# A streamed decode-attention kernel: one A head's V per set moves from TensorE to GpSimd and VectorE, the softmax minimum reaches all rows by one product, and the stream is walked in another order

## The chip, the cores and the metric

The kernel runs on one core of a Trainium2 chip. The metric is the device time of one execution in microseconds (us). Engines: PE is TensorE, DVE is VectorE, ACT is ScalarE, POOL is GpSimd, SP is SyncE, whose queue issues the transfers. All data are fp32.

## What is computed

One query row `x` (448 wide) goes through two attention blocks with cached keys and values, and a sigmoid gate mixes the two outputs:

```
A: 16 heads, each with its own K and V (8192 rows x 256)
B: 16 query heads on 8 K/V heads (two query heads share one K/V)
per block:  q = x @ wq;  p = softmax(q . K * 256**-0.5);  o = p @ V;  y = concat(o) @ wo
g = sigmoid(sum(x * gate_w));   out = g * yA + (1 - g) * yB
```

K and V are 24 + 24 arrays of 8 MB, about 403 MB of the 432 MB that are read; the rest are `wq` and `wo`. Each element is used for one or two products, so the work is a stream.

## The kernel before

The work is cut into 8 sets (`s`). A set has two A heads (`r` = 0 and 1) and one B head (`r` = 2, with two query rows). Each K and each V is cut into 4 tiles (`t`) of 128 partitions x 4096 elements (16 cache rows of 256 in each partition). A set also has one `wq` item (its columns of both query weights) and one `wo` item (its rows of both output weights). The last set's `wo` is cut into `first` and `rest`. The names below are like v7.0.3: V, set 7, head 0, tile 3; k6.1.3 is the last key tile of head 1 of set 6.

The list `order()` writes the items one after another, and this is the order in which the host has laid them in DRAM, in which they are loaded, and in which the instructions of every engine stand. The stream is loaded without regard to item borders, in *fills* of 16384 elements a partition (8.39 MB, four tiles), into a ring of three slots (`load`, L112 to L119; SP's queue). There are 53 fills, numbered 0 to 52: 50 full ones (0 to 49), one of 6144 elements (fill 50, 3072 KB), and two cut into five parts each (fill 51: the last V tiles and `first`; fill 52: `rest`). Fill n+3 goes into the slot of fill n, and its load waits until everything that reads or writes fill n there is done. The first three loads are issued at once.

What each item costs on the engines:

- A keys (`scores_a`, L232): DVE multiplies the tile by q in place (L239; q lies in PSUM) and sums each row of 256 (L240). After the last tile the smallest of the 64 scores of each partition (`low`, L243).
- B keys (`scores_b`): the tile lies transposed, and PE multiplies it by q (8 products of 512 columns a tile, each two instructions in the trace); after the last tile DVE takes `low` from PSUM (L258).
- `softmax` (L261), after the last key tile of a head: PE turns `low` into one row (`ident`), DVE takes its minimum (L269), PE spreads that to all rows (`ones`, or `alt` for B's two query rows), ACT copies it (L277) and takes the exponential (L281, L288). For B, DVE then transposes the weights (L283).
- V (`attend`): PE, 8 products a tile (`o<-slot,p` or `o<-slot,pr`), summed in PSUM. After the last tile come `sums` (sum of the weights over all partitions by PE, its reciprocal on DVE, L300), `take` (ACT copies the PSUM, L333) and one item later `narrow` (PE adds up the four row groups, `sm<-pick_a,ob`, and DVE scales, L349).
- `wo`: `emit` adds the set's eight 448-wide products to `Y` in PSUM. After that of set 6, `quarters` copies `Y` (DVE, L367) and folds it to four rows.

PE and DVE are in order: an instruction that waits holds everything behind it on its engine.

Of the kernel before, what the change touches and what calls it, by code (L numbers as in the profile page):

```python
# [36 lines left out]
TAIL = [[11 * UNIT, 10 * UNIT, EARLY * D + 2 * UNIT, 4 * UNIT, 2 * UNIT], [2 * D, D, D, 336, 112]]  # L37


def order():  # L40

    out = [("wq", 0, 0, 0)]
    for s in range(NS):
        def k(r, *ts):
            return [("k", s, r, t) for t in ts]

        def v(r, *ts, of=s):
            return [("v", of, r, t) for t in ts]

        if s == 0:  # L50
            out += k(0, 0) + k(2, 0, 1) + k(0, 1) + k(2, 2) + k(0, 2) + k(2, 3) + k(0, 3)
            out += v(2, 0, 1) + k(1, 0) + v(2, 2, 3) + k(1, 1) + v(0, 0, 1) + k(1, 2) + v(0, 2)
            out += k(1, 3) + v(0, 3) + [("wq", 1, 0, 0)]
            continue
        out += k(0, 0) + v(1, 0, 1, of=s - 1) + k(0, 1) + v(1, 2, 3, of=s - 1)
        out += k(0, 2) + k(2, 0, 1) + k(0, 3) + k(2, 2, 3) + [("wo", s - 1, 0, 0)]
        out += k(1, 0) + v(0, 0, 1) + k(1, 1) + v(0, 2, 3)
        if s < NS - 1:
            out += [("wq", s + 1, 0, 0)] + k(1, 2) + v(2, 0, 1) + k(1, 3) + v(2, 2, 3)
        else:  # L60
            out += k(1, 2) + v(2, 0) + k(1, 3) + v(2, 1, 2, 3) + v(1, 0, 1, 2)
            out += [("first", s, 0, 0)] + v(1, 3) + [("rest", s, 0, 0)]
    return out
# [14 lines left out]
def kernel(  # L78
# [21 lines left out]
    def mm(o, l, r, start=False, stop=False):  # L100
        nc.tensor.matmul(o, l, r, start=start, stop=stop, skip_group_check=True)  # L101
# [130 lines left out]
    def scores_a(s, r, t, a):  # L232
        if t == 0:
            S[s, r] = small.tile([P, NT * ROWS], F32, name="s", bufs=3)
        q = QA[s][:, r * DH:(r + 1) * DH]
        for d, n, v in pieces(a, TILE):
            j, n = d // DH, n // DH
            v = v.rearrange("p (j d) -> p j d", d=DH)
            nc.vector.tensor_tensor(v, v, q[:, None, :].to_broadcast([P, n, DH]), op=OP.mult)  # L239
            nc.vector.tensor_reduce(S[s, r][:, t * ROWS + j:t * ROWS + j + n], v, axis=AX.X, op=OP.add)  # L240
        if t == NT - 1:
            low = small.tile([P, 1], F32, name="low")
            nc.vector.tensor_reduce(low, S[s, r], axis=AX.X, op=OP.min)  # L243
            OF[s, r] = low

    def scores_b(s, t, a):
        if t == 0:
            SC[s] = ps_sc.tile([P, UNIT], F32, name="sc")
        sc = SC[s]
        for d, n, v in pieces(a, TILE):  # L250
# [5 lines left out]
        if t == NT - 1:  # L256
            low = small.tile([P, 1], F32, name="low")
            nc.vector.tensor_reduce(low, sc, axis=AX.X, op=OP.min)  # L258
            OF[s, 2] = low

    def softmax(s, r):  # L261
        turned = ps_s.tile([1, P], F32, name="sm")
        mm(turned, OF.pop((s, r)), ident, start=True, stop=True)
        m = 2 if r == 2 else 1
        least = small.tile([1, 2], F32, name="least")
        view = turned
        if r == 2:
            view = turned.rearrange("p (g r) -> p g r", g=NG)[:, :, :R].rearrange("p g (t m) -> p m g t", m=2)
        nc.vector.tensor_reduce(least[:, :m], view, axis=AX.XY if r == 2 else AX.X, op=OP.min)  # L269
        all_rows = ps_s.tile([P, 1], F32, name="sm")  # L270
        if r == 2:
            for k in range(2):
                mm(all_rows, alt[:, k], least[:, k:k + 1], start=(k == 0), stop=(k == 1))
        else:
            mm(all_rows, ones[:1, :], least[:, :1], start=True, stop=True)
        bias = small.tile([P, 1], F32, name="bias")
        nc.scalar.activation(bias, all_rows, AF.Copy)  # L277
        rs = small.tile([P, 1], F32, name="rs", bufs=4)
        if r == 2:
            px = small.tile([P, UNIT], F32, name="px")  # L280
            nc.scalar.activation(px, SC.pop(s), AF.Exp, bias=bias, scale=-1.0, accum_out=rs)  # L281
            pr = small.tile([P, UNIT], F32, name="pr", bufs=1)
            nc.vector.transpose(pr.rearrange("p (q r k) -> p q k r", r=BLK, k=2),  # L283
                                px.rearrange("p (q k c) -> p q k c", c=BLK, k=2))
            PR[s, r] = pr
        else:
            p = small.tile([P, NT * ROWS], F32, name="p")
            nc.scalar.activation(p, S.pop((s, r)), AF.Exp, bias=bias, scale=-1.0, accum_out=rs)  # L288
            PR[s, r] = p
        RS[s, r] = rs  # L290

    def sums(s, r):
# [4 lines left out]
        for k in range(m):
            mm(z[:, k:k + 1], par[:, k] if r == 2 else ones, rs, start=True, stop=True)
# [6 lines left out]
    def attend(s, r, t, a):  # L305
        if t == 0:
# [4 lines left out]
        for d, n, v in pieces(a, TILE):  # L311
            for b in range(d // UNIT, (d + n) // UNIT):
                g = b % NG
                c = b * UNIT - d
# [75 lines left out]
    nxt = SLOTS  # L390
    gone = 0
    last = len(items) - 1
    for i, ((kind, s, r, t), a) in enumerate(items):
        if kind == "wq":
            qrow = queries(s, a)
            after(i, turn, s, qrow)
        elif kind == "k":
            if r == 2:
                scores_b(s, t, a)
            else:  # L400
                scores_a(s, r, t, a)
            if t == NT - 1:
                softmax(s, r)
        elif kind == "v":
            attend(s, r, t, a)
            if t == NT - 1:
                end = i == last - 1
                if not end:
# [1 line left out]
                take(s, r, 2 if end else 1)  # L410
                if not end:
                    after(i + 1, narrow, s, r)
        elif kind == "wo":
# [102 lines left out]
```

## Time and profile before

| | |
|---|---|
| three runs | 1010.61 us median (1009.96 to 1010.9) |
| the profiled execution | 1009.79 us, span 1007.7 us |
| read from DRAM | 432.02 MB, 429 GB/s over the span |
| PE busy / mean granted clock | 492.8 us (49%) / 0.725 |
| DVE busy | 596.9 us (59%) |
| ACT, POOL busy | 37.9 us, 0.7 us |
| chain that ended last | DMA 61%, DVE 22%, PE 16% of the span |

The profile is of one execution, whose span is 2.1 us shorter than its time and whose time is 0.8 us under the median of the three runs. The numbers of the groups in it (lines of the kernel, engine, output and inputs, partitions x elements) have a mean duration in ns. In a timeline row the first number is the start, the second the time from there to the end of the row's last instruction; in square brackets is how long the engine had been idle and what ended that. A stage row has, after the length, busy time and number of instructions on PE, PEld (its weight loads), DVE, ACT and POOL, then the granted PE clock, the DMA share and GB/s.

### The profile page before, as it was taken

The numbers are of one execution on the slowest core, as the hardware profiler recorded it, in microseconds if no ns is written. First come the engines' busy times: TensorE is split into PE (matmuls) and PEld (weight loads), VectorE is DVE, ScalarE is ACT, GpSimd is POOL, SyncE is SP. The second block draws the span as 40 slices with busy tenths as digits, with TensorE's granted clock in tenths as the row PEclk, the third lists the DMA queues.
The fourth block names the chain that finished last, engine by engine and source line by source line (L and its number), as shares of the span: only waits on it lengthen the run. The fifth ranks groups of instructions, "written<-read, shape, count | busy, mean of one in ns | idle before, by whom it ended". The sixth has DMA issues, their size and how long they took to land.

```text
span 1007.7 us, 6321 instructions
## 1 busy us (share of the span) xinstructions
PE 492.8 (49%) x2843; PEld 148.1 (15%) x2843; DVE 596.9 (59%) x294; ACT 37.9 (4%) x107; POOL 0.7 (0%) x6
## 2 busy tenths in 40 slices
PE   1615482554435563445442566345634366544628
PEld 0201120111111211011110121111211112111102
DVE  1686767527766467652776646755277762675581
ACT  0000000000000000000000000000000000000000
POOL 0000000000000000000000000000000000000000
PEclk9857686777777777577777776766767677776658
DMA  9999999999999999999999999999999999999997
GB/s 416 416 455 419 443 425 424 447 427 442 425 425 442 432 435 440 432 430 427 440 430 445 427 440 425 430 442 422 453 420 440 430 432 440 424 448 427 432 418 296
DMA packets 8962, 432.42 MB, mean 429 GB/s; under 512 B 1256, under 2 KB 1640, under 8 KB 1896
## 3 DMA queue, kind: packets, MB, share of 16 engines
q1 hardware_dynamic: 8792, 432.02, 99.1%
q8 instruction: 22, 0.36, 0.1%
q14 instruction: 4, 0.03, 0.0%
q10 hardware_dynamic: 144, 0.00, 0.0%
HBM read 432.02 MB, written 0.00 MB: 429 GB/s over the span
## 4 chain that ended last, share of the span: by engine, by line
DMA 61%; DVE 22%; PE 16%; issue 0%; ACT 0%; SPq 0%
DMA slot<-in_stream_dram 61%; DVE s L240 11%; DVE slot L239 11%; PE o L101 6%; PE sc L101 4%; PE sm L101 3%; PE q L101 3%; DVE least L269 0%; DVE low L243 0%; PE Y L101 0%; DVE qb L230 0%; ACT px L281 0%; DVE pr L283 0%; DVE low L258 0%; ACT qrow L222 0%
## 5 line engine op out<-in xcount | busy, mean ns | idle before, releaser
L239 DVE TENSOR_TENSOR slot<-slot,q 128x4096 f32<-128x4096 f32 (+6 forms) x78 | 284.1, 3642 | 70.2 <-DMA slot<-in_stream_dram 70.2
L240 DVE TENSOR_REDUCE s<-slot 128x16 f32<-128x4096 f32 (+6 forms) x78 | 285.0, 3654 | 2.7
L101 PE MATMUL o<-slot,p 128*2 128x512 f32 (+1 forms) x1028 | 162.2, 743 | 185.5 <-DMA slot<-in_stream_dram 185.5
L101 PE MATMUL sc<-slot,qb 128*32 128x512 f32 x512 | 98.0, 857 | 68.1 <-DMA slot<-in_stream_dram 67.8
L101 PE MATMUL sm<-ident,low 128*1 128x128 f32 x48 | 13.0, 369 | 180.5 <-DVE low L243 162.0
L101 PE MATMUL o<-slot,pr 128*4 128x512 f32 x512 | 84.0, 773 | 29.1 <-DMA slot<-in_stream_dram 28.9
L300 DVE RECIPROCAL rz<-sm 128x1 f32<-128x1 f32 (+1 forms) x24 | 4.0, 167 | 130.4 <-PE sm L101 130.4
L101 PEld LDWEIGHTS o<-slot,p 128*2 128x2 f32 x1028 | 29.5, 97 | 301.6 <-DMA slot<-in_stream_dram 199.8
L349 DVE TENSOR_TENSOR ocs<-sm,rz 128x2 f32<-128x2 f32 (+2 forms) x25 | 3.9, 154 | 73.5 <-PE sm L101 73.4
L258 DVE TENSOR_REDUCE low<-sc 128x1 f32<-128x512 f32 x8 | 5.5, 690 | 63.8 <-PE sc L101 63.8
L101 PE MATMUL q<-slot,xr 128*128 128x512 f32 (+1 forms) x80 | 33.5, 567 | 11.7 <-DMA slot<-in_stream_dram 11.7
L101 PEld LDWEIGHTS sc<-slot,qb 128*32 128x32 f32 x512 | 20.2, 146 | 128.7 <-DMA slot<-in_stream_dram 77.3
L101 PEld LDWEIGHTS sm<-ident,low 128*1 128x1 f32 x48 | 2.3, 80 | 206.2 <-issue 96.0
L101 PE MATMUL sc<-slot,xr 128*1 128x512 f32 (+1 forms) x80 | 30.2, 525 | 0.0
L333 ACT ACTIVATE ob<-o 128x512 f32<-128x512 f32 (+1 forms) x24 | 14.1, 588 | 396.4 <-PE o L101 396.4
L101 PEld LDWEIGHTS o<-slot,pr 128*4 128x4 f32 x512 | 14.7, 100 | 84.0 <-issue 48.7
L277 ACT ACTIVATE bias<-sm 128x1 f32<-128x1 f32 x24 | 4.1, 171 | 477.0 <-PE sm L101 477.0
L101 PEld LDWEIGHTS q<-slot,xr 128*128 128x128 f32 x80 | 16.3, 214 | 25.7 <-DMA slot<-in_stream_dram 12.6
L101 PE MATMUL sm<-pick_a,ob 128*128 128x1 f32 x124 | 17.2, 259 | 3.1 <-ACT ob L333 2.9
L101 PE MATMUL Y<-slot,ocs 128*1 128x448 f32 (+3 forms) x178 | 17.3, 505 | 0.0
L101 PEld LDWEIGHTS sm<-pick_a,ob 128*128 128x128 f32 x124 | 15.9, 200 | 7.1 <-ACT ob L333 4.0
L269 DVE TENSOR_REDUCE least<-sm 1x1 f32<-1x128 f32 (+1 forms) x24 | 5.9, 245 | 16.0 <-PE sm L101 16.0
(64 smaller groups left out, 136.3 us busy)
## 6 DMA issues: line engine op xcount, KB each, us to landing
slot<-in_stream_dram SPq DMA_DIRECT2D x1, 3072.0 KB, 26.4
slot<-in_stream_dram SPq DMA_DIRECT2D x1, 2816.0 KB, 16.7
slot<-in_stream_dram SPq DMA_DIRECT2D x1, 2560.0 KB, 22.4
slot<-in_stream_dram SPq DMA_DIRECT2D x1, 1184.0 KB
slot<-in_stream_dram SPq DMA_DIRECT2D x1, 1024.0 KB, 26.7
slot<-in_stream_dram SPq DMA_DIRECT2D x50, 40.4
slot<-in_stream_dram SPq DMA_DIRECT2D x1, 512.0 KB, 27.5
slot<-in_stream_dram SPq DMA_DIRECT2D x1, 448.0 KB, 10.5
```

The lines of the kernel that those rows point to most:

```text
L101: nc.tensor.matmul(o, l, r, start=start, stop=stop, skip_group_check=True)
L239: nc.vector.tensor_tensor(v, v, q[:, None, :].to_broadcast([P, n, DH]), op=OP.mult)
L240: nc.vector.tensor_reduce(S[s, r][:, t * ROWS + j:t * ROWS + j + n], v, axis=AX.X, op=OP.add)
L258: nc.vector.tensor_reduce(low, sc, axis=AX.X, op=OP.min)
L269: nc.vector.tensor_reduce(least[:, :m], view, axis=AX.XY if r == 2 else AX.X, op=OP.min)
L277: nc.scalar.activation(bias, all_rows, AF.Copy)
L300: nc.vector.reciprocal(rz[:, :m], z[:, :m])
L333: nc.scalar.activation(ob[k][:, :n], o[:, k * n:(k + 1) * n], AF.Copy)
L349: nc.vector.tensor_tensor(ocs[:, e, :m], oc[e.start][:, e, :m], z.to_broadcast([P, e.stop - e.start, m]), op=OP.mult)
```

## The change

It has four parts.

1. V of one A head a set is no longer multiplied on PE. For the heads in `SPREAD` (head 0 of set 0, head 1 of sets 0 to 6: 8 heads, 32 tiles) POOL multiplies the tile in place by the weights (`spread`), and DVE later sums the 16 rows of each partition to 256 numbers (`settle`, reading with a step of 256 elements) and adds them to the head's `acc`. `settle` runs where a fill ends in the program, and ahead of each `wo`. `gather` then lets PE add up the partitions of `acc` in two products. The other 8 A heads and B stay with `attend`.
2. In `softmax` one product, whose stationary side is `low` repeated to 128 columns, puts all 128 values into every row; DVE takes each row's minimum straight from PSUM as the bias. For B it takes two minima a row and picks one by a mask (`half`). The second product and ACT's copy are gone. In `sums`, B takes one product of two columns in place of two.
3. `order()` deals the tiles of a set from three lists (A keys, PE's tiles, and V of the `SPREAD` head) by a string, so that they alternate. `wo` and `wq` of a set move near its end. The last six items (the four V tiles of head 1 of set 7, with `first` ahead of the fourth and `rest` behind it) keep their places, and so do the borders of the fills.
4. The loop walks an item that crosses from one fill into the next as two items, so that the load into the old slot and the `settle` of that fill stand between the two.

```diff
+SPREAD = {(0, 0)} | {(s, 1) for s in range(NS - 1)}
 def order():
...
-        out += k(0, 0) + v(1, 0, 1, of=s - 1) + k(0, 1) + v(1, 2, 3, of=s - 1)
...
+        walk = "kfkfkfkfkfvkfvkfvqkfv" if s == 0 else "kfkfvfkfkvfkfkvfkvfkfffof" if last else "kfkfvfkfvfkfvfkfvfkfkfoqkf"
+        for c in walk:
+            if c in "oq":
+                out.append(("wo", s - 1, 0, 0) if c == "o" else ("wq", s + 1, 0, 0))
+            else:
+                out.append({"k": keys, "f": fill, "v": mine}[c].pop(0))
...
     def softmax(s, r):
-        turned = ps_s.tile([1, P], F32, name="sm")
-        mm(turned, OF.pop((s, r)), ident, start=True, stop=True)
...
-            mm(all_rows, ones[:1, :], least[:, :1], start=True, stop=True)
-        bias = small.tile([P, 1], F32, name="bias")
-        nc.scalar.activation(bias, all_rows, AF.Copy)
+        every = ps_s.tile([P, P], F32, name="sm")
+        mm(every, OF.pop((s, r)).to_broadcast([P, P]), ident, start=True, stop=True)
+        bias = small.tile([P, 1], F32, name="bias")
         if r == 2:
...
+            nc.vector.tensor_reduce(least, view, axis=AX.XY, op=OP.min)
+            nc.vector.tensor_tensor(least, least, half, op=OP.mult)
+            nc.vector.tensor_reduce(bias, least, axis=AX.X, op=OP.add)
         else:
+            nc.vector.tensor_reduce(bias, every, axis=AX.X, op=OP.min)
...
+    def spread(s, r, t, a, lo, size):
...
+        for d, n, v in pieces(a + lo, size):
+            j, n = (lo + d) // DH, n // DH
+            w = PR[s, r][:, t * ROWS + j:t * ROWS + j + n]
+            v = v.rearrange("p (j d) -> p j d", d=DH)
+            nc.gpsimd.tensor_tensor(v, v, w[:, :, None].to_broadcast([P, n, DH]), op=OP.mult)
+            todo.append((s, r, v))
+    def settle():
+        for s, r, v in todo:
+            first = not ACC[s, r]
+            acc = small.tile([P, DH], F32, name="acc" if first else "more")
+            nc.vector.tensor_reduce(acc, v.rearrange("p j d -> p d j"), axis=AX.X, op=OP.add)
+            if first:
+                ACC[s, r].append(acc)
+            else:
+                nc.vector.tensor_tensor(ACC[s, r][0], ACC[s, r][0], acc, op=OP.add)
+        todo.clear()
+    def gather(s, r):
...
+        for e in range(2):
+            mm(oc[:, e, :1], acc[:, e * P:(e + 1) * P], gs[:, 0:1], start=True, stop=True)
...
         elif kind == "wo":
+            settle()
+            for r in range(2):
+                if (s, r) in SPREAD:
+                    sums(s, r)
+                    gather(s, r)
             emit(s, a)
...
-        while gone < len(ends) and a + SIZE[kind] >= ends[gone]:
+        while gone < len(ends) and a + lo + n >= ends[gone]:
             gone += 1
+            settle()
             if nxt < len(FILLS):
                 load(nxt)
```

What the fills hold near the end shows the new order best. Before, fills 46 to 49 hold: k7.2.0 (end), k7.2.1, k7.0.3, k7.2.2, k7.2.3 (start) | k7.2.3, wo6, k7.1.0, v7.0.0, v7.0.1 | v7.0.1 (end), k7.1.1, v7.0.2, v7.0.3, k7.1.2 (7/8) | k7.1.2 (end), v7.2.0, k7.1.3, v7.2.1, v7.2.2. Now fills 43 to 49 hold: v6.0.2, wo5, wq7, k6.1.3, v6.0.3 (3/4) | v6.0.3 (end), k7.0.0, k7.2.0, k7.0.1, k7.2.1 | k7.2.1 (end), v6.1.0, k7.2.2, k7.0.2, k7.2.3 | k7.2.3 (end), k7.0.3, v6.1.1, v7.2.0, k7.1.0 (3/4) | k7.1.0 (end), v7.2.1, k7.1.1, v6.1.2, v7.2.2 | v7.2.2 (end), k7.1.2, v7.2.3, v6.1.3, k7.1.3 (3/4) | k7.1.3 (end), v7.0.0, v7.0.1, v7.0.2, wo6. Fill 50 holds v7.2.2 (end), v7.2.3, v7.1.0 (3/8) before and wo6 (end), v7.0.3, v7.1.0 (3/8) now; fills 51 and 52 are the same.

DVE before, from the key tiles in fill 48 to the last softmax's minimum (`slot` is a tile in the ring, `s` the scores, `ocs` a head's finished output):

```order
L239 TENSOR_TENSOR slot<-slot,q 128x3584
L240 TENSOR_REDUCE s<-slot 128x14
L239 TENSOR_TENSOR slot<-slot,q 128x512
L240 TENSOR_REDUCE s<-slot 128x2
L349 TENSOR_TENSOR ocs<-sm,rz 128x2
L239 TENSOR_TENSOR slot<-slot,q 128x4096
L240 TENSOR_REDUCE s<-slot 128x16
L243 TENSOR_REDUCE low<-s 128x1
L269 TENSOR_REDUCE least<-sm 1x1
```

DVE now, fill 48 (k7.1.2, B's `sums` and output, three quarters of k7.1.3, the sum of v6.1.3) and what follows to the last softmax's minimum:

```order
L232 TENSOR_TENSOR slot<-slot,q 128x4096
L233 TENSOR_REDUCE s<-slot 128x16
L288 TENSOR_SCALAR both<-half,rs 128x2
L292 RECIPROCAL rz<-sm 128x2
L375 TENSOR_TENSOR ocs<-sm,rz 128x4
L232 TENSOR_TENSOR slot<-slot,q 128x3072
L233 TENSOR_REDUCE s<-slot 128x12
L338 TENSOR_REDUCE more<-slot 128x256
L342 TENSOR_TENSOR acc<-acc,more 128x256
L232 TENSOR_TENSOR slot<-slot,q 128x1024
L233 TENSOR_REDUCE s<-slot 128x4
L236 TENSOR_REDUCE low<-s 128x1
```

The last key tile's first three quarters have moved from fill 49 into fill 48, and ahead of its last quarter stand the sum over a tile that POOL has weighed and an addition. The same sum and addition stand at the end of fills 46 and 47, and the sum at that of fill 45.

PE before, from the last softmax (`sm<-ident,low`, `sm<-least,ones`) on:

```order
L101 MATMUL sm<-ident,low 1x128
L101 MATMUL sm<-least,ones 128x1
L101 MATMUL o_125<-slot,pr 4x512 x24
L101 MATMUL sm<-rs,par 128x1 x2
L101 MATMUL o_126<-slot,p 2x512 x8
L101 MATMUL sm<-pick_b,ob 128x2 x4
L101 MATMUL o_126<-slot,p 2x512 x16
L101 MATMUL sm<-rs,ones 128x1
L101 MATMUL Y<-slot,ocs 1x112 x12
L101 MATMUL o_126<-slot,p 2x512 x6
L101 MATMUL o_126<-slot,p 2x256 x4
```

PE now, from the same softmax (`sm<-ident,low`) to `quarters` (`Y<-ysum`) and the narrowing of head 0; behind it come `o_120<-slot,p` x21 and then the same rows as before from `sm<-rs,ones` on:

```order
L100 MATMUL sm<-ident,low 128x128
L100 MATMUL o_119<-slot,p 2x512 x24
L100 MATMUL sm<-rs,ones 128x1
L100 MATMUL sm<-gs,acc 128x1 x2
L100 MATMUL Y<-slot,ocs 1x448 x6
L100 MATMUL Y<-slot,ocs 1x384
L100 MATMUL Y<-slot,ocs 1x64
L100 MATMUL Y<-slot,ocs 1x448
L100 MATMUL o_119<-slot,p 2x512 x8
L100 MATMUL sm<-rs,ones 128x1
L100 MATMUL o_120<-slot,p 2x512 x3
L100 MATMUL Y<-ysum,row_of 1x112 x4
```

The whole of set 6's `wo`, with `gather` ahead of it and `quarters` behind, and one V tile more now stand behind the last softmax on PE; before, `wo` of set 6 stood ahead of the first tile of k7.1.

More of the change, by code (lines that the diff above doesn't have):

```diff
@@ L43, in order @@
     for s in range(NS):
[L44 to L54, printed above, removed]
-        out += k(0, 0) + v(1, 0, 1, of=s - 1) + k(0, 1) + v(1, 2, 3, of=s - 1)
[L56 to L63, printed above, removed]
+        fill = [("k", s, 2, t) for t in range(NT)] + [("v", s, 2, t) for t in range(NT)]
+        mine = [("v", s, 0, t) for t in range(NT)]
+        if s:
+            fill += mine
+            mine = [("v", s - 1, 1, t) for t in range(NT)]
+        keys = [("k", s, r, t) for r in range(2) for t in range(NT)]
+        last = s == NS - 1
+        walk = "kfkfkfkfkfvkfvkfvqkfv" if s == 0 else "kfkfvfkfkvfkfkvfkfvkfffof" if last else "kfkfvfkfvfkfvfkfvfkfkfoqkf"
+        for c in walk:
[3 more added lines that the diff above has]
+                out.append({"k": keys, "f": fill, "v": mine}[c].pop(0))
+        assert not keys + fill + mine
+    s = NS - 1
+    return out + [("v", s, 1, t) for t in range(NT - 1)] + [("first", s, 0, 0), ("v", s, 1, NT - 1), ("rest", s, 0, 0)]
 SIZE = {"wq": 2 * WQ, "wo": WO, "first": EARLY * D, "rest": WO - EARLY * D, "k": TILE, "v": TILE}
@@ L261, in softmax @@
     def softmax(s, r):
[L262 to L277 removed]
+        every = ps_s.tile([P, P], F32, name="sm")
+        mm(every, OF.pop((s, r)).to_broadcast([P, P]), ident, start=True, stop=True)
+        bias = small.tile([P, 1], F32, name="bias")
+        if r == 2:
+            least = small.tile([P, 2], F32, name="least")
+            view = every.rearrange("p (g r) -> p g r", g=NG)[:, :, :R].rearrange("p g (t m) -> p m g t", m=2)
+            nc.vector.tensor_reduce(least, view, axis=AX.XY, op=OP.min)
+            nc.vector.tensor_tensor(least, least, half, op=OP.mult)
+            nc.vector.tensor_reduce(bias, least, axis=AX.X, op=OP.add)
+        else:
+            nc.vector.tensor_reduce(bias, every, axis=AX.X, op=OP.min)
         rs = small.tile([P, 1], F32, name="rs", bufs=4)
@@ L296, in sums @@
         z = ps_s.tile([P, 2], F32, name="sm")
-        for k in range(m):
-            mm(z[:, k:k + 1], par[:, k] if r == 2 else ones, rs, start=True, stop=True)
+        if r == 2:
+            both = small.tile([P, 2], F32, name="both")
+            nc.vector.tensor_scalar(both, half, rs, None, op0=OP.mult)
+            rs = both
+        mm(z[:, :m], ones, rs, start=True, stop=True)
         rz = small.tile([P, 2], F32, name="rz", bufs=3)
@@ L310, in attend @@
         w = 4 if r == 2 else 2
-        for d, n, v in pieces(a, TILE):
+        for d, n, v in pieces(a + lo, size):
+            d += lo
             for b in range(d // UNIT, (d + n) // UNIT):
@@ L326, in attend @@
                    stop=(t == NT - 1 and b >= NG))
+    todo, ACC = [], {}
+    def spread(s, r, t, a, lo, size):
+        if t == lo == 0:
+            ACC[s, r] = []
+        for d, n, v in pieces(a + lo, size):
+            j, n = (lo + d) // DH, n // DH
+            w = PR[s, r][:, t * ROWS + j:t * ROWS + j + n]
[13 more added lines that the diff above has]
+    def gather(s, r):
+        acc = ACC.pop((s, r))[0]
+        oc = ps_s.tile([P, 2, 2], F32, name="sm")
+        for e in range(2):
+            mm(oc[:, e, :1], acc[:, e * P:(e + 1) * P], gs[:, 0:1], start=True, stop=True)
+        ocs = small.tile([P, 2, 2], F32, name="ocs", bufs=6)
+        nc.vector.tensor_tensor(ocs[:, :, :1], oc[:, :, :1], RZ.pop((s, r))[:, None, :1].to_broadcast([P, 2, 1]), op=OP.mult)
+        OC[s, r] = ocs
     def take(s, r, parts=1):
@@ L345, in narrow @@
                start=(k == 0), stop=(k == 1))
-        ocs = small.tile([P, 2, 2], F32, name="ocs", bufs=4)
+        ocs = small.tile([P, 2, 2], F32, name="ocs", bufs=6)
         z = RZ.pop((s, r))[:, None, :m]
@@ L376, in emit_block @@
                     mm(Y[BLK * g:BLK * g + 1, lo - g * YN:hi - g * YN], l(), v[:, lo - d:hi - d])
+    ends = [s + sum(f) for s, f in zip(starts, FILLS)]
     items, a = [], 0
     for it in order():
-        items.append((it, a))
-        a += SIZE[it[0]]
+        size, lo = SIZE[it[0]], 0
+        while lo < size:
+            n = size - lo
+            if it[0] in "kv":
+                n = min([n] + [e - a - lo for e in ends if e > a + lo])
+            items.append((it, a, lo, n))
+            lo += n
+        a += size
     assert a == TOTAL
-    ends = [s + sum(f) for s, f in zip(starts, FILLS)]
     later = {}
@@ L392 @@
     last = len(items) - 1
-    for i, ((kind, s, r, t), a) in enumerate(items):
+    for i, ((kind, s, r, t), a, lo, n) in enumerate(items):
+        done = (t, lo + n) == (NT - 1, TILE)
         if kind == "wq":
-            qrow = queries(s, a)
-            after(i, turn, s, qrow)
+            turn(s, queries(s, a))
         elif kind == "k":
             if r == 2:
-                scores_b(s, t, a)
+                scores_b(s, t, a, lo, n)
             else:
-                scores_a(s, r, t, a)
-            if t == NT - 1:
+                scores_a(s, r, t, a, lo, n)
+            if done:
                 softmax(s, r)
         elif kind == "v":
[L405 to L408, printed above, removed]
+            if (s, r) in SPREAD:
+                spread(s, r, t, a, lo, n)
+            else:
+                attend(s, r, t, a, lo, n)
+                if done:
+                    end = i == last - 1
+                    if not end:
+                        sums(s, r)
+                    take(s, r, 2 if end else 1)
+                    if not end:
+                        after(i + 1, narrow, s, r)
+        elif kind == "wo":
+            settle()
+            for r in range(2):
+                if (s, r) in SPREAD:
                     sums(s, r)
[L410 to L413, printed above, removed]
+                    gather(s, r)
             emit(s, a)
```

33 lines of the change are left out of this document (13 added, 20 removed).

## The prediction

> **What bounds the kernel now.** I read the stage rows first, then SP's waits and the loads, then the timeline of the end. First: a stage row over the middle of the run, SP's wait for DVE (total, times, longest), the loads (median us from issue to landing), the first load in the chain, and two stage rows of the end.
>
> ```profile
> 100.00:960.00 860.00, 429.53 (x2408) 126.20 (x2408) 515.09 (x231) 31.87 (x91) 0.00 (x0) 0.72 1.00 434
> SPq L117 <- DVE s L240: 897.9, 50, 41.7
> slot<-in_stream_dram SPq DMA_DIRECT2D x50, 40.4
> 0.74 22.08 DMA slot<-in_stream_dram
> 1001.00:1002.00 1.00, 1.00 (x16) 0.27 (x14) 0.00 (x0) 0.00 (x0) 0.00 (x0) 1.00 0.41 148
> 1002.00:1003.00 1.00, 0.91 (x22) 0.39 (x18) 0.00 (x0) 0.40 (x2) 0.00 (x0) 1.00 0.20 57
> ```
>
> For 860 us the DMA share is 1.00 at 434 GB/s: a fill of 8.39 MB takes 19.3 us, and no engine can make the stream end earlier. SP waits 898 us for DVE, but that is no loss. A load lands 40.4 us after its issue, so its slot came free 3 x 19.3 - 40.4 = 17.5 us after that slot's own data had landed. The first load took 22.1 us for 19.3 us of data, 2.8 us of start; so up to 2 x 19.3 - 2.8 = 35.8 us would still keep the queue filled. The stream dries up between 1001 and 1003 us. What can change the time is the end, or a slot that comes free more than some 36 us late.
>
> Second, the timeline of the end:
>
> ```profile
> 970.91 2.23 SPq L117 DMA_DIRECT2D slot<-in_stream_dram  x5
> 973.49 0.69 DVE L239 TENSOR_TENSOR slot<-slot,q 128x512 f32<-128x512 f32 x1 [2.65 <-DMA slot<-in_stream_dram]
> 979.33 4.42 DVE L240 TENSOR_REDUCE s<-slot 128x16 f32<-128x4096 f32 x1
> 983.78 0.22 DVE L243 TENSOR_REDUCE low<-s 128x1 f32<-128x64 f32 x1
> 984.06 0.59 PE L101 MATMUL sm<-ident,low 128*1 128x128 f32 x2 [6.95 <-DVE low L243]
> 985.53 6.97 PE L101 MATMUL o<-slot,pr 128*4 128x512 f32 x48
> 992.96 1.90 PE L101 MATMUL o<-slot,p 128*2 128x512 f32 x16
> 994.79 1.05 PE L101 MATMUL sm<-pick_b,ob 128*128 128x2 f32 x8
> 995.77 3.62 PE L101 MATMUL o<-slot,p 128*2 128x512 f32 x32
> 999.32 0.38 PE L101 MATMUL sm<-rs,ones 128*128 128x1 f32 x2
> 999.63 0.76 PE L101 MATMUL Y<-slot,ocs 128*1 128x112 f32 x24
> 1000.20 2.10 PE L101 MATMUL o<-slot,p 128*2 128x512 f32 x18
> 1002.14 0.39 PE L101 MATMUL o<-slot,p 128*2 128x256 f32 x2
> 1002.60 0.38 ACT L333 ACTIVATE ob<-o 128x256 f32<-128x256 f32 x1 [9.43 <-PE o L101]
> 1004.87 0.28 DVE L438 COPY ys<-Y 128x112 f32<-128x112 f32 x1 [0.58 <-PE Y L101]
> ```
>
> Fill 49 lands at 973.5 with the last key tile. DVE needs until 984.0 for it, the softmax frees PE at 985.5, and PE then works without a gap until 1002.5: 17.0 us that had piled up behind the softmax. So the end is a chain: DVE, PE, and 5.2 us of closing steps to 1007.7. The sum below moves "PE free" and "PE done".
>
> **The change part by part.** Prices, from the groups by shape:
>
> ```profile
> L240 DVE TENSOR_REDUCE s<-slot 128x16 f32<-128x4096 f32 x50 | 221.0, 4420 | 1.7
> L239 DVE TENSOR_TENSOR slot<-slot,q 128x4096 f32<-128x4096 f32 x50 | 220.4, 4408 | 42.9 <-DMA slot<-in_stream_dram 42.9
> L258 DVE TENSOR_REDUCE low<-sc 128x1 f32<-128x512 f32 x8 | 5.5, 690 | 63.8 <-PE sc L101 63.8
> L281 ACT ACTIVATE px<-sc,bias 128x512 f32<-128x512 f32 x8 | 5.5, 688 | 0.3
> L283 DVE STREAM_TRANSPOSE pr<-px 128x512 f32<-128x512 f32 x8 | 5.7, 713 | 15.3 <-ACT px L281 15.3
> L269 DVE TENSOR_REDUCE least<-sm 1x1 f32<-1x128 f32 x16 | 4.5, 278 | 11.6 <-PE sm L101 11.6
> L147 POOL IOTA ident<- 128x128 f32 x1 | 0.2, 243 | 0.4 <-POOLq L502 0.4
> L150 POOL IOTA rows<- 128x64 f32 x1 | 0.3, 253 | 0.0
> ```
>
> A key tile is 4.41 + 4.42 us and a gap, 8.9 us on DVE (6.7 for three quarters, 2.4 for one).
>
> *The sum over a weighed tile.* No row reads with a step of 256 elements. From below it is 4.4 us: the same instruction over the same 4096 elements. From above I take 8.8 us, product and sum of a key tile together. I take 4.4, since L240 differs in the order of reading alone. [...] Here 32 sums add 32 x 4.4 = 141 us to DVE and the additions some 9 (0.4 each, between L269 and L258): 747 of 1008 us, so DVE isn't full over the run.
>
> *POOL's product.* The nearest rows are POOL's two iotas: 1.9 ns a column by the wider one (7.8 us a tile), 4.0 by the narrower (16.2); from below DVE's 4.4. I take 7.8, the wider tile being nearer. No fill holds more than one tile's worth, so POOL keeps pace up to 19 us. In fills 45 to 48 DVE comes to the sum 13 us or more after landing: free up to there; 16.2 would cost under 1 us.
>
> *PE's V work* of 32 tiles goes; PE waits for the stream in the middle, so nothing comes of it. *The softmax* loses a product and a copy: 0.9 us each, off the path but for the last. *The fills walked in parts*: SP waits for the readers of the slot before and now, nothing. *`gather`* is two products, 0.6 us, twice what `sm<-rs,ones` took in the end's timeline.
>
> *The order.* Now the end, fill by fill, with DVE in order. The landings stay: 857.6 for fill 43, and 19.3 more each. Rows for it (landing of fills 43, 45, 46, 48; `wq`; `wo`; `quarters`):
>
> ```profile
> 843.04 3.69 PE L101 MATMUL q<-slot,xr 128*128 128x512 f32 x10
> 846.65 3.60 PE L101 MATMUL sc<-slot,xr 128*1 128x512 f32 x10
> 851.16 1.05 PE L101 MATMUL sm<-ones,qrow 1*128 1x1 f32 x8
> 857.58 2.75 PE L101 MATMUL o<-slot,pr 128*4 128x512 f32 x20 [3.55 <-DMA slot<-in_stream_dram]
> 896.28 5.50 PE L101 MATMUL o<-slot,p 128*2 128x512 f32 x32 [13.08 <-DMA slot<-in_stream_dram]
> 915.57 4.42 DVE L239 TENSOR_TENSOR slot<-slot,q 128x4096 f32<-128x4096 f32 x1 [4.43 <-DMA slot<-in_stream_dram]
> 939.45 3.17 PE L101 MATMUL Y<-slot,ocs 128*1 128x448 f32 x16
> 950.63 0.55 PE L101 MATMUL Y<-ysum,row_of 128*1 128x112 f32 x8 [5.30 <-DVE ysum L367]
> 954.19 4.42 DVE L239 TENSOR_TENSOR slot<-slot,q 128x4096 f32<-128x4096 f32 x1 [3.61 <-DMA slot<-in_stream_dram]
> ```
>
> - Fill 43: PE does half of v6.0.2 (1.2), `sums` and `gather` (1.0), wo5 (3.2), wq7 (7.2) and the turn of q with ACT's copy (2.0): 872.2. Only then DVE gets to k6.1.3: 881.1; `low`, product, minimum 1.1: 882.2. Next on DVE is a reciprocal that waits for PE's v6.0.3 (2.8) and its sum (0.4) behind that product: 885.4.
> - Fill 44: two key tiles, 903.2. Fill 45: a key tile and a sum, 916.5.
> - Fill 46, landed at 915.6: B's softmax 3.5 (0.7 + 0.6 for PE + three small steps 0.5 + ACT 1.0 + 0.7), a key tile 8.9, a softmax 1.2, 6.7, sum and addition 4.8: 941.6.
> - Fill 47: 2.4 + 8.9 + 4.8: 957.7.
> - Fill 48, landed at 954.2: 8.9; B's mask, reciprocal and output with two round trips to PE 1.8; 6.7; 4.8: 979.9.
> - Fill 49: 2.4, `low` 0.2, PE's product 0.7: PE is free at 983.2, 2.3 us sooner than the 985.5 before.
>
> But more stands behind it. PE then has 24 products (7.0, as before after its idle time), `sums` and `gather` 1.0, wo6 1.6 (16 instructions at the 0.113 us that 3.62 / 32 gives, 448 of 512 wide), v7.0.3 1.9, `sums` 0.4, `quarters` 0.55, narrowing 1.05, 24 products of v7.1 5.4 (1.5 x 3.62), `sums` 0.4, `first` 0.6, the last 2.3: 22.2 us in place of 17.0. PE is done at 1005.4, **2.9 us later**. The span becomes 1010.6, the execution 1012.7; the profiled one stood 0.8 under the median, so the forecast is **1013.5 us**.
>
> Late next is slot 48: it came free at 970.9 and now at 979.9. What is queued then, fill 50 of 3.1 MB behind fill 49, lasts until 973.5 + 7.2 = 980.7; with 2.8 us of start the queue is empty for up to 2.0 us, and the stream ends at 1005 at most. PE, done at 1005.4, and the last `Y` after 1007 cover it. Without PE's lag it would cost those 2.0.
>
> **The rivals.**
> 1. *The sum with a step is dearer.* It counts four times on the path (fills 45 to 48; DVE has no gap between them). In the middle of the bounds, 6.6 us, the end moves by 8.8: 1022.3. At 8.8 us it moves by 17.6, and early slots come late too (fill 3 holds 1.9 key tiles and a sum, 25 us against 19.3; some 4 us): 1035. For it: no row covers the step. Against it: L283 writes every second word and costs 713 ns beside 690 for L258's 512 elements.
> 2. *DVE waits for POOL.* In fill 46 DVE multiplies two SBUF tiles (`least`, `half`) at 918.3, while POOL multiplies v6.1.1 from 915.6 to 923.4. If DVE stands until POOL is done, everything moves by 5.1: 1018.6. [...] No row shows it, as POOL does nothing here.
> 3. *Not slower.* My waits in fills 43 and 48 (3.2 + 1.8 us) fold away, because PE is ahead. It decides from 2.9 us on: then PE is free at 980.3. If DVE has caught up when fill 49 lands, PE is free at 976.8 and done at 999.0, and the stream's last V part, some 2.6 us ahead of its end, sets 1000.8 in place of 1002.5: 1008.9.
> 4. *POOL over 19 us a tile.* Then it paces the stream through runs of five tiles, well past 1040. The iotas speak against it.
>
> **Chances.** Forecast as worked out 0.42; rival 1 0.30; rival 2 0.13; rival 3 0.11; rival 4 0.04. The forecast's own range is 1010.5 to 1017. The range of all, 1009 to 1031, leaves out the dearest third of rival 1, rival 4, and a little of rival 3. A difference under 0.2% (2 us) can't be told from none here. Faster by more: only the best of rival 3, 0.04. Within: the rest of it, and a third of the forecast's case, whose middle is 0.3%: 0.21. Slower: 0.75.
>
> **What would show it.** The DMA share stays at 1.00 to about 975. The group `acc`/`more<-slot` shows the sum's price at once, 4.4 or more; POOL's group its own. DVE should have no idle time for the stream from 885 to 980; the load after fill 50 should go out near 980; PE's `sm<-ident,low` of the last softmax should come near 982.5, and its work without a gap should run to 1005. The forecast is wrong if DVE catches up before fill 49 (then the end is the stream's), or if the sum is over 5 us.

## Result, and the profile after

| | before | after |
|---|---|---|
| median of the runs | 1010.33 us (1009.96 to 1010.9) | 1072.49 us (1071.78 to 1073.74) |
| ratio to before | 1 | 1.0616 [1.0598, 1.0634] |
| span of the profiled execution | 1007.7 us | 1070.9 us |
| DVE busy | 596.9 us (59%) | 862.1 us (81%) |

The kernel became 62 us slower. The forecast was 1013.5 us (1009 to 1031): the sign was right, the size was not.

Read first, on the page of after: the busy times, the DMA share in 40 slices, the chain of work that ended last, and the median load.

```profile
PE 422.0 (39%) x2223; PEld 134.2 (13%) x2223; DVE 862.1 (81%) x382; ACT 29.0 (3%) x75; POOL 226.0 (21%) x42
DMA  9999897999989999999989999999999999999837
DVE 80%; PE 16%; DMA 2%; ACT 1%; issue 1%; ACTq 0%; DVEq 0%
slot<-in_stream_dram SPq DMA_DIRECT2D x50, 24.9
```

Before, the chain was 61% DMA and 22% DVE; now it is 80% DVE and 2% DMA. A load lands 24.9 us after its issue instead of 40.4: a fill itself takes 19.3 us, so a load found 21 us of earlier work in the queue before and finds under 6 now. Slots come free that much later, and the stream has lost its reserve.

Where the stream stands still is read from stage rows of after (columns as in the prediction: length, PE, PEld, DVE, ACT, POOL, granted clock, DMA share, GB/s):

```profile
100.00:300.00 200.00, 74.22 (x362) 26.18 (x366) 172.64 (x73) 5.07 (x13) 50.05 (x9) 0.63 0.89 378
300.00:500.00 200.00, 75.66 (x410) 22.74 (x406) 174.23 (x86) 5.26 (x14) 48.87 (x10) 0.65 0.99 425
500.00:700.00 200.00, 86.85 (x448) 27.57 (x442) 160.21 (x62) 5.07 (x13) 35.47 (x6) 0.69 0.98 420
700.00:900.00 200.00, 83.02 (x416) 24.60 (x412) 171.50 (x66) 5.26 (x14) 48.80 (x7) 0.68 1.00 430
1025.00:1040.00 15.00, 1.31 (x7) 1.23 (x6) 13.61 (x4) 0.00 (x0) 0.00 (x0) 0.50 0.00 0
```

Before, the DMA share was 1.00 from 100 to 960 us. Now it is 0.89 in the first stretch (about 22 us lost there), 0.98 to 1.00 in the next three, and near the end there are 15 us without a byte. Counted by fill from the packets of both traces, the stream is 5 us late at fill 6, 27 at fill 14, 40 at fill 45, 46 at fill 49 and 63 at fill 51.

Why DVE is late shows in three views of after. First the groups by shape (the sum, the addition, the pick of B's minimum, POOL's product):

```profile
L338 DVE TENSOR_REDUCE more<-slot 128x256 f32<-128x4096 f32 x21 | 149.5, 7117 | 0.0
L338 DVE TENSOR_REDUCE acc<-slot 128x256 f32<-128x4096 f32 x7 | 49.0, 7006 | 0.0
L342 DVE TENSOR_TENSOR acc<-acc,more 128x256 f32<-128x256 f32 x28 | 26.1, 931 | 1.0
L263 DVE TENSOR_TENSOR least<-least,half 128x2 f32<-128x2 f32 x8 | 13.2, 1650 | 0.3
L331 POOL TENSOR_TENSOR slot<-slot,p 128x4096 f32<-128x4096 f32 x28 | 196.6, 7022 | 662.5 <-DMA slot<-in_stream_dram 264.8 <-ACT p L277 241.7 <-PE o L100 84.5
```

The sum with a step takes 7.0 us where the prediction took 4.4. The two small DVE instructions with two SBUF inputs have means far above their size, and the timeline says why (start, duration):

```profile
73.66 7.02 POOL L331 TENSOR_TENSOR slot<-slot,p 128x4096 f32<-128x4096 f32 x1 [72.38 <-ACT p L277]
78.22 2.48 DVE L263 TENSOR_TENSOR least<-least,half 128x2 f32<-128x2 f32 x1
121.39 7.02 POOL L331 TENSOR_TENSOR slot<-slot,p 128x4096 f32<-128x4096 f32 x1 [13.09 <-DMA slot<-in_stream_dram]
122.96 5.74 DVE L342 TENSOR_TENSOR acc<-acc,more 128x256 f32<-128x256 f32 x1
146.15 5.98 DVE L342 TENSOR_TENSOR acc<-acc,more 128x256 f32<-128x256 f32 x1
840.09 4.24 DVE L263 TENSOR_TENSOR least<-least,half 128x2 f32<-128x2 f32 x1
970.13 0.16 DVE L263 TENSOR_TENSOR least<-least,half 128x2 f32<-128x2 f32 x1
996.01 0.42 DVE L342 TENSOR_TENSOR acc<-acc,more 128x256 f32<-128x256 f32 x1
```

POOL's products end at 80.68 and 128.41; the DVE instructions that began beside them end at 80.70 and 128.70. With POOL idle the same instructions take 0.16 and 0.42 us. Over the run this standing behind POOL is 13.2 - 8 x 0.16 = 11.9 us for L263 and 26.1 - 28 x 0.42 = 14.3 us for L342. It falls on few instructions: three additions, the last at 173.17, and five of the eight picks, the last at 840.09. All other additions and picks take their 0.42 and 0.16 us.

Third, DVE's waits (total, times, longest) and one of them in the timeline:

```profile
DVE qb L223 <- PE sm L100: 83.0, 7, 12.8
DVE rz L292 <- PE sm L100: 42.8, 18, 6.7
280.71 0.16 DVE L223 COPY qb<-sm 128x4 f32<-128x4 f32 x1 [12.24 <-PE sm L100]
```

At seven borders of sets DVE stands some 12 us, until PE has worked through the next set's `wq`, for a copy of 0.16 us; the last key tile of the old set stands behind it on DVE. No row of DVE's waits names the stream any more.

Last, the end of after, DVE and PE:

```profile
1014.90 4.42 DVE L232 TENSOR_TENSOR slot<-slot,q 128x4096 f32<-128x4096 f32 x1
1033.08 7.00 DVE L338 TENSOR_REDUCE more<-slot 128x256 f32<-128x4096 f32 x1
1040.11 0.42 DVE L342 TENSOR_TENSOR acc<-acc,more 128x256 f32<-128x256 f32 x1
1042.95 0.22 DVE L236 TENSOR_REDUCE low<-s 128x1 f32<-128x64 f32 x1
1043.23 0.80 PE L100 MATMUL sm<-ident,low 128*128 128x128 f32 x2 [16.91 <-DVE low L236]
1043.95 6.75 PE L100 MATMUL o<-slot,p 128*2 128x512 f32 x48
1065.24 0.39 PE L100 MATMUL o<-slot,p 128*2 128x256 f32 x2
```

DVE is through with fill 47 at 1014.9; the forecast had 957.7, so 57 of the 59 us of the miss are there before the part that it worked out most closely. Fill 48 then takes 25.6 us where the forecast had 22.2, and PE's work behind the last softmax takes 21.7 us (1043.95 to 1065.63) where it had 22.2.

### The profile page after: what moved, and what is told of

The parts are those of the page before. It is cut to its first block, busy times and chain, and to the rows that moved or that the text cites. A ratio compares the mean times of both kernels' runs of the same rounds, so it can differ in the third digit from the quotient of the medians.

```text
span 1070.9 us, 5256 instructions
## 1 busy us (share of the span) xinstructions
PE 422.0 (39%) x2223; PEld 134.2 (13%) x2223; DVE 862.1 (81%) x382; ACT 29.0 (3%) x75; POOL 226.0 (21%) x42
## 4 chain that ended last, share of the span: by engine, by line
DVE 80%; PE 16%; DMA 2%; ACT 1%; issue 1%; ACTq 0%; DVEq 0%
DVE s L233 27%; DVE slot L232 26%; DVE more L338 16%; PE sm L100 5%; DVE acc L338 5%; PE o L100 3%; PE q L100 3%; PE sc L100 3%; DVE acc L342 2%; DMA xs<-in_small_dram 2%; PE Y L100 1%; DVE least L263 1%; ACT px L270 1%; DVE pr L272 1%; DVE low L252 0%
## 5 line engine op out<-in xcount | busy, mean ns | idle before, releaser
L331 POOL TENSOR_TENSOR slot<-slot,p 128x4096 f32<-128x4096 f32 (+1 forms) x36 | 225.3, 6262 | 777.4 <-ACT p L277 311.6
L233 DVE TENSOR_REDUCE s<-slot 128x16 f32<-128x4096 f32 (+4 forms) x80 | 285.3, 3566 | 2.8
L232 DVE TENSOR_TENSOR slot<-slot,q 128x4096 f32<-128x4096 f32 (+4 forms) x80 | 284.4, 3555 | 0.0
L338 DVE TENSOR_REDUCE more<-slot 128x256 f32<-128x4096 f32 (+1 forms) x28 | 175.1, 6252 | 0.0
L100 PE MATMUL sm<-ident,low 128*128 128x128 f32 x48 | 18.7, 493 | 323.7 <-DVE low L236 206.2
L100 PE MATMUL sc<-slot,qb 128*32 128x512 f32 x512 | 78.9, 743 | 57.8 <-DMA slot<-in_stream_dram 57.5
L100 PE MATMUL o<-slot,p 128*2 128x512 f32 (+1 forms) x516 | 86.6, 803 | 23.2 <-DMA slot<-in_stream_dram 23.2
L338 DVE TENSOR_REDUCE acc<-slot 128x256 f32<-128x4096 f32 (+1 forms) x8 | 52.6, 6578 | 0.0
L100 PE MATMUL Y<-slot,ocs 128*1 128x448 f32 (+4 forms) x182 | 30.6, 629 | 23.7 <-DVE ocs L351 23.7
L100 PEld LDWEIGHTS o<-slot,pr 128*4 128x4 f32 x512 | 14.3, 104 | 115.5 <-issue 56.2
L342 DVE TENSOR_TENSOR acc<-acc,more 128x256 f32<-128x256 f32 x28 | 26.1, 931 | 1.0
## 6 DMA issues: line engine op xcount, KB each, us to landing
slot<-in_stream_dram SPq DMA_DIRECT2D x50, 24.9
```

What stands on the lines that cost most here:

```text
L331: nc.gpsimd.tensor_tensor(v, v, w[:, :, None].to_broadcast([P, n, DH]), op=OP.mult)
L338: nc.vector.tensor_reduce(acc, v.rearrange("p j d -> p d j"), axis=AX.X, op=OP.add)
L342: nc.vector.tensor_tensor(ACC[s, r][0], ACC[s, r][0], acc, op=OP.add)
```

## Experiments

Four theories: **S**, the sum's step of 256 elements; **P**, DVE standing behind POOL; **B**, DVE idle at the borders of sets; **O**, the new order, walk and softmax by themselves. Of S, P and B only what exceeds the 19.3 us of a fill on DVE's chain can cost time.

**Adjacent rows (tests S).** The host lays the V tiles of the `SPREAD` heads so that the 16 rows of a column are neighbours; POOL and DVE do the same work.

```diff
-            v = v.rearrange("p (j d) -> p j d", d=DH)
-            nc.gpsimd.tensor_tensor(v, v, w[:, :, None].to_broadcast([P, n, DH]), op=OP.mult)
+            v = v.rearrange("p (d j) -> p d j", j=ROWS)
+            nc.gpsimd.tensor_tensor(v, v, w[:, None, :].to_broadcast([P, n, ROWS]), op=OP.mult)
...
-            nc.vector.tensor_reduce(acc, v.rearrange("p j d -> p d j"), axis=AX.X, op=OP.add)
+            nc.vector.tensor_reduce(to, v, axis=AX.X, op=OP.add)
```

> The changed kernel with the V tiles of the weighed heads laid out by the host so that the 16 numbers to be summed are adjacent; POOL's product and DVE's sum and additions keep their sizes. The sum should fall from 7.02 us to 4.4 us a tile, 32 x 2.6 = 84 us of DVE's 862. If the step is the main cause (theory S): 1011 to 1018 us. If DVE's standing behind POOL decides (theory P: its 28 additions and 8 masks take 39 us where 13 would do): over 1040. If DVE's idling at the border of each set decides (theory B: the copy of q waits 83 us for PE): over 1040.

Measured: 1023.1 us, ratio 1.0131 [1.0116, 1.0146]. Groups and one stage row:

```profile
L338 DVE TENSOR_REDUCE more<-slot 128x256 f32<-128x4096 f32 x21 | 92.5, 4405 | 0.0
L340 DVE TENSOR_TENSOR acc<-acc,more 128x256 f32<-128x256 f32 x21 | 55.7, 2650 | 0.7
L331 POOL TENSOR_TENSOR slot<-slot,p 128x4096 f32<-128x4096 f32 x28 | 248.3, 8869 | 584.5 <-DMA slot<-in_stream_dram 438.1 <-ACT p L277 125.2 <-DVE s L233 10.8
100.00:300.00 200.00, 78.52 (x410) 26.16 (x410) 172.93 (x79) 5.07 (x13) 67.37 (x10) 0.67 1.00 429
```

The sum falls to 4.4 us, and 49 us of time go with it, though the additions now stand longer behind POOL, whose product became longer too. The share of the first stretch is 1.00 again. S is the largest single cause, but 13 us remain.

**Nothing with two SBUF inputs beside POOL (tests P).** PE adds the parts of a head in `gather`, and B's minimum is picked with scalars.

```diff
-                nc.vector.tensor_tensor(ACC[s, r][0], ACC[s, r][0], acc, op=OP.add)
+            ACC[s, r].append(acc)
...
-            mm(oc[:, e, :1], acc[:, e * P:(e + 1) * P], gs[:, 0:1], start=True, stop=True)
+            for k, acc in enumerate(accs):
+                mm(oc[:, e, :1], acc[:, e * P:(e + 1) * P], gs[:, 0:1], start=(k == 0), stop=(k == len(accs) - 1))
...
-            nc.vector.tensor_tensor(least, least, half, op=OP.mult)
-            nc.vector.tensor_reduce(bias, least, axis=AX.X, op=OP.add)
+            nc.vector.tensor_scalar(odd, least[:, 1:2], half[:, 1:2], None, op0=OP.mult)
+            nc.vector.tensor_scalar(bias, least[:, 0:1], half[:, 0:1], odd, op0=OP.mult, op1=OP.add)
```

> The changed kernel without a DVE instruction that reads two SBUF tensors beside POOL: PE adds up the parts of a weighed head in its gather (up to 8 products in place of 1 for each half), and two pointer scalars pick B's minimum. DVE loses 39 us of 862, the sum with a step stays at 7.0 us. Theory P: 1012 to 1020 us. Theory S: over 1050. Theory B: over 1055.

Measured: 1043.82 us, 1.033 [1.0312, 1.0347], 28.7 us under after, with the sum still at 7.1 us. The stage row of the first stretch:

```profile
100.00:300.00 200.00, 85.81 (x434) 31.72 (x434) 169.84 (x71) 5.07 (x13) 52.90 (x9) 0.64 0.95 409
```

0.95 instead of 0.89: P is a real part of the early loss.

**The turn of q later (tests B).** The next set's `wq` is turned into columns two items later, so that the old set's key tile stands ahead of the copy on DVE.

```diff
-            turn(s, queries(s, a))
+            after(i + 2 if i else i, turn, s, queries(s, a))
```

> The changed kernel with one step moved: q of the next set is turned and copied to SBUF two items later, behind the last key tile of the set, so that DVE works on that tile while PE does wo and wq. Theory B: the 83 us of waiting go to under 20 and the time to 1012 to 1025 us. Theories S and P: 1060 or more, since DVE stays the bound by its own work.

Measured: 1043.59 us (1036.64 to 1046.44), 1.0321 [1.0283, 1.0359]. The wait for `qb`, the additions and the first stretch:

```profile
DVE qb L223 <- PE sm L100: 21.0, 8, 10.5
L342 DVE TENSOR_TENSOR acc<-acc,more 128x256 f32<-128x256 f32 x28 | 42.6, 1523 | 1.0
100.00:300.00 200.00, 79.85 (x410) 27.20 (x410) 181.77 (x76) 5.07 (x13) 51.57 (x9) 0.65 0.94 398
```

62 us of waiting go, 28.9 us of time; part came back as standing behind POOL (additions 26.1 to 42.6 us). After fill 15 the stream falls no further behind, where after still loses 13 us from there to fill 45. This creeping loss isn't B's alone: with adjacent rows (above) it is gone too, though the waits for `qb` stand there (81.9 us), and without P it is 6 us. S and B are both needed for it, and P makes up half.

**V back on PE (tests O).** `SPREAD` is empty; the order, the walk in parts, the softmax and the sums stay. There are three PSUM tiles for heads in place of two and one small one in place of two. The two halves of the last head's output share one small tile, and part of this kernel's output isn't right; its products on V are as many as before the change (1020 instructions for A, 512 for B).

```diff
-SPREAD = {(0, 0)} | {(s, 1) for s in range(NS - 1)}
+SPREAD = set()
...
-            OF[s, r] = len(turns) % 2
+            OF[s, r] = len(turns) % 3
```

> The changed kernel with all V on PE again (no head is weighed by POOL; three PSUM tiles for outputs in place of two, one small PSUM tile in place of two): order, softmax and the walk in parts stay. If POOL's and DVE's new work is the whole loss: 1009 to 1013 us. If the new order itself loses (theory O): over 1025.

Measured: 1009.38 us, 0.9996 [0.9986, 1.0005]: no difference. DVE waits for the stream again (the last line is from before the change):

```profile
DVE slot L232 <- DMA slot<-in_stream_dram: 88.0, 17, 10.0
DVE qb L223 <- PE sm L100: 113.4, 8, 20.7
DVE qb L230 <- PE sm L101: 18.3, 8, 12.6
```

The order, the walk and the softmax cost nothing by themselves; all 62 us come with V on POOL and DVE. But the waits of B belong to the new order: 113 us here, 18.3 before the change. They are harmless while DVE has time to wait for the stream as well.

**S and P together.** Adjacent rows, and each tile's sum kept apart for PE to add.

```diff
-            nc.vector.tensor_reduce(to, v, axis=AX.X, op=OP.add)
-            if t:
-                nc.vector.tensor_tensor(acc, acc, to, op=OP.add)
+            nc.vector.tensor_reduce(ACC[s, r][t][:, d:d + n], v, axis=AX.X, op=OP.add)
```

> The two edits together: the 16 numbers of a sum adjacent, and no DVE instruction with two SBUF tensors beside POOL. This is the case that the prediction's sum was made for (4.4 us a sum, no standing behind POOL): 1013.5 us by it. By theory T (DVE's own work, its standing behind POOL and its idling for PE add up on DVE's chain, and only what exceeds the stream's 19.3 us a fill counts): 1011 to 1015, with nothing lost before fill 46. If POOL's product, 8.9 us with adjacent rows in place of 7.0, holds the sums up: over 1018.

Measured: 1018.98 us, 1.0083 [1.0067, 1.0099], above what was expected. The waits at the borders are all still there:

```profile
DVE qb L223 <- PE sm L100: 90.2, 7, 17.1
```

By the packets this kernel loses 8 us at the end, and the one without them (below) 4 to 5: B counts there too, which I had left out. The other reading given ahead of the run, that POOL's longer product holds the sums up, doesn't fit: none of DVE's waits names POOL here, and the kernel with all three edits has the same product (8.88 us in both) and is 4.5 us faster.

**P and B together**, the sum still with its step:

```diff
-            turn(s, queries(s, a))
+            after(i + 2 if i else i, turn, s, queries(s, a))
...
-                nc.vector.tensor_tensor(ACC[s, r][0], ACC[s, r][0], acc, op=OP.add)
+            ACC[s, r].append(acc)
```

> The sum with a step stays (7.0 us); no DVE instruction with two SBUF tensors beside POOL, and q is turned two items later. This leaves the step as the only one of the three costs. Rival 1's term of the prediction gives 1013.5 + 4 x 2.6 = 1024 for it; by theory T 1022 to 1030, with the loss in the first fills and at the end and none between. If the three costs don't add up but the step alone keeps DVE behind: over 1035.

Measured: 1029.21 us, 1.0184 [1.0169, 1.0198], as expected. By the packets it loses 8 us in the early fills, none in the middle and 13 at the end. This is the price of 7.0 us in place of 4.4 when nothing else is wrong: 1029.2 - 1014.5 (next run) = 14.7 us.

**All three.**

```diff
-            nc.vector.tensor_reduce(acc, v.rearrange("p j d -> p d j"), axis=AX.X, op=OP.add)
-                nc.vector.tensor_tensor(ACC[s, r][0], ACC[s, r][0], acc, op=OP.add)
-            turn(s, queries(s, a))
+            nc.vector.tensor_reduce(ACC[s, r][t][:, d:d + n], v, axis=AX.X, op=OP.add)
+            after(i + 2 if i else i, turn, s, queries(s, a))
```

> All three edits: adjacent rows, no standing behind POOL, q turned two items later. Theory T: DVE has 740 us of work and waits for the stream again, 1009 to 1014 us, at most the tail's 3 us over the kernel before. If something else in the weighing by POOL costs time: over 1016.

Measured: 1014.49 us (1014.28 to 1015.01), 1.0041 [1.0025, 1.0057]. DVE's wait for the stream, the median load, a stage row, and the end on DVE and PE:

```profile
DVE slot L232 <- DMA slot<-in_stream_dram: 77.0, 23, 10.1
slot<-in_stream_dram SPq DMA_DIRECT2D x50, 40.1
100.00:300.00 200.00, 94.13 (x452) 31.50 (x452) 166.28 (x80) 5.84 (x15) 72.04 (x11) 0.66 1.00 434
975.03 4.41 DVE L337 TENSOR_REDUCE part<-slot 128x256 f32<-128x4096 f32 x1
981.86 0.22 DVE L236 TENSOR_REDUCE low<-s 128x1 f32<-128x64 f32 x1
982.86 6.42 PE L100 MATMUL o<-slot,p 128*2 128x512 f32 x48
1006.84 0.39 PE L100 MATMUL o<-slot,p 128*2 128x256 f32 x2
```

The stream is whole again (share 1.00, loads 40.1 us), and the end is the forecast's: PE free at 982.9 (forecast 983.2), 1014.5 us (forecast 1013.5). PE is done at 1007.2 instead of 1005.4, among other things because `gather` has 16 small instructions here (1.9 us). Ahead of fill 46 DVE waits 7.8 us for B's scores, so that the forecast's steps for fills 43 to 45 aren't tested by this kernel.

The savings don't add: S, P and B alone saved 49.4, 28.7 and 28.9 us, 107 in sum, and 58.0 together. A saving counts only while DVE is later than the stream: here DVE waits 77 us for the stream, which it never did in the changed kernel.

**The last keys earlier.** If the end is DVE, then PE behind it, the last A keys should come sooner. Before, with the new softmax and sums, and the last set's stream written in this order:

```diff
+        if s == NS - 1:
+            out += k(0, 2) + k(2, 0, 1) + k(0, 3) + k(2, 2) + k(1, 0) + k(2, 3) + [("wo", s - 1, 0, 0)]
+            out += v(0, 0) + k(1, 1) + v(0, 1) + k(1, 2) + v(0, 2) + k(1, 3) + v(0, 3) + v(2, 0, 1, 2, 3) + v(1, 0, 1, 2)
+            out += [("first", s, 0, 0)] + v(1, 3) + [("rest", s, 0, 0)]
+            continue
```

> Not the changed kernel but the one before, with the changed softmax and with the last set's A keys moved up, so that only an eighth of the last key tile lies in fill 49 (k7.1.0 in fills 46 and 47, k7.1.1 in 47, k7.1.2 and k7.1.3 in 48). PE should be free from the last softmax near 976 in place of 985.5 and not work off a backlog at the end; the end is then the stream's, 1000.8 in place of 1002.5 for the last V part: 1.0 to 2.5 us faster than before (0.1 to 0.25%). If the end isn't bound by that backlog: the same. If slot 48, free at 972 to 975 in place of 970.9, leaves the queue empty: the same or 1 us slower.

Measured: 1008.4 us (1008.01 to 1008.8), 0.998 [0.9971, 0.9989]. This beats both kernels, though by 0.2% only. PE now waits for the last data, where before it had 17 us of work piled up:

```profile
994.46 2.74 PE L106 MATMUL o<-slot,p 128*2 128x512 f32 x20 [1.46 <-DMA slot<-in_stream_dram]
999.57 1.04 PE L106 MATMUL o<-slot,p 128*2 128x512 f32 x8 [0.53 <-DMA slot<-in_stream_dram]
1001.84 0.56 PE L106 MATMUL Y<-slot,ocs 128*1 128x112 f32 x16 [0.45 <-DMA slot<-in_stream_dram]
```

**Which of the two parts did it.** The softmax and sums alone on before:

```diff
-        turned = ps_s.tile([1, P], F32, name="sm")
-        mm(turned, OF.pop((s, r)), ident, start=True, stop=True)
+        every = ps_s.tile([P, P], F32, name="sm")
+        mm(every, OF.pop((s, r)).to_broadcast([P, P]), ident, start=True, stop=True)
```

> Before, with the changed softmax and sums alone: the least copied into both halves, one subtraction over 256 columns, one product for the minimum of all rows. Of DVE's row on the end chain about 0.5 us goes per fill, and the PE product that spreads the minimum takes some 0.1 us more. If the gain of the moved keys with the new softmax (2.0 us) came from the softmax, this run is 1.0 to 2.0 us faster than before; if it came from the keys, it is within 0.9 us of before.

and the moved keys alone (the diff of the last keys, without the softmax):

```diff
+        if s == NS - 1:
+            out += k(0, 2) + k(2, 0, 1) + k(0, 3) + k(2, 2) + k(1, 0) + k(2, 3) + [("wo", s - 1, 0, 0)]
...
```

> Before, with the last set's A keys moved up in the stream alone, softmax and sums as before. If the gain of 2.0 us came from the keys, this run is 1.2 to 2.2 us faster than before; if from the softmax, it is within 0.9 us of before.

(The first of these expectations describes its edit wrongly: as the diff shows, it is the changed kernel's softmax, one product and a minimum in each row, with no subtraction.)

Measured: softmax alone 1009.25 us, 0.9991 [0.9982, 1.0]; keys alone 1008.52 us, 0.9983 [0.9974, 0.9992]. The gain comes from the keys: 1.7 of the 2.0 us. The softmax's 1.0 us lies at the edge of what these runs can tell from none, and with the keys moved it adds 0.1 to 0.3 us at most: its place on the end chain is then gone.

## Why the prediction was wrong, and where it was right

- **The sum over a weighed tile: failed.** "I take 4.4, since L240 differs in the order of reading alone." It measured 7.0 us, 1.71 ns a column, and the order of reading was the price: 4.4 us again with adjacent rows (4405 ns, 1.08 ns a column). Of the bounds 4.4 to 8.8 I took the lower one, with no row of DVE reading that way.
- **"DVE isn't full over the run": failed, and this is most of the miss.** With the right 7.0 us the working would still have given some 1024 us (1013.5 + 4 x 2.6), since it let a sum count "four times on the path", in fills 45 to 48, and took the landings from before. DVE's 747 us became 862: 227.7 for the sums instead of 141, 26.1 for the additions instead of 9, and 13.2 for L263. With 12 us of idling at each border, DVE's chain is longer than 19.3 us a fill from fill 5 on: counted from the packets, 20.4 us a fill on average from there to fill 49. So the landings, which the working kept from before ("The landings stay"), moved with DVE. An average over 1008 us says nothing on runs of fills that hold two key tiles and a sum. I worked out one early fill (25 us against 19.3, under rival 1 only) and stopped there.
- **DVE waits for POOL: right in kind (rival 2), wrong in place and count.** I priced it once, at B's minimum in fill 46, 5.1 us, an estimate, as no row showed DVE standing; just there it didn't happen (0.16 us at 970.13, since DVE came too late to meet POOL). It happened at three additions in the first 180 us and at five of the eight minima up to 844 us, 26 us in sum. DVE's end follows POOL's by 0.02 and 0.29 us in the two pairs shown. Only DVE is held up: POOL's products of 4096 elements all take 7.02 us. The key products (one input in PSUM) keep 4408 ns in both kernels, and the 15 of 48 that run beside a POOL product are no longer than the others (4.38 to 4.41 us).
- **The wait at a border: seen once, not carried over.** My sum for fill 43 had "only then DVE gets to k6.1.3" (872.2), but the same string of the walk makes the same wait at seven borders, 83 us in all, and I counted none of the others.
- **Slot 48: failed as a consequence.** "Up to 2.0 us" of empty queue, covered by PE's lag, became 15 us and more, since the slot came free some 69 us later than before (near 1040) instead of 9.
- **Right:** PE's pile behind the last softmax (22.2 us, measured 21.7); POOL's product (7.8, measured 7.02) keeping pace, though 7.8 was read from an iota, another instruction, so that its nearness is partly luck; the softmax and the walk in parts, taken at nothing; and the end chain from fill 46 on, which the kernel without the three costs follows to 0.3 us at PE's release. That its time is only 1.0 us over the forecast is partly luck: its span is 1.9 us over (1012.5 against 1010.6), and its profiled run stood 0.2 us under the median, not 0.8.

Of my theories none holds alone: each of the three single edits came out between the time that its own theory gave and the time that the others gave. S is the largest, and P or B alone takes away nearly half of what is lost. What stays open: P's own price with S and B already gone was not run, so the 58 us can't be shared out exactly, and adjacent rows also made POOL's product longer (8.9 us), which lengthens P.

## What to carry to other kernels

When work moves onto an engine that had slack on average, add up its work for each period of the stream, waits included, and not only at the end: here the stream was late from fill 6 on (5 us), long before fill 43, where my working began. A price without a row in the trace deserves a small run or its upper end, above all when it is paid 32 times. And an order that is dealt by a pattern repeats its faults at every border: a wait seen at one place should be counted at all of them.

## What was not expected of the hardware

- POOL's product of 4096 elements took 7.02 us where one weight serves 256 neighbouring elements (1.71 ns a column) and 8.87 us with adjacent rows, where the weights change at every element (2.17 ns).
- A two-element DVE instruction took up to 4.24 us, and a 256-element one up to 5.98, in place of 0.16 and 0.42, for beginning beside a POOL product.
- The product that turns `low` takes longer with a stationary side repeated to 128 columns: 0.80 us for its two instructions at a granted clock of 0.50, against 0.59 before at the same clock. It costs the end chain 0.2 us, and saves the second product and the copy.
